# A linear-attention and long-convolution kernel: six batches' stores on GpSimd's queue, the first keys as fp32 by SyncE, sine's table first, three batches' keys and queries crossed

## The chip, the cores and the metric

The kernel runs on one core of a Trainium2 chip. Its metric is the device time in microseconds of one execution. The engines are named as in the profile: PE (TensorE's matrix products; PEld are its weight loads), DVE (VectorE), ACT (ScalarE), POOL (GpSimd) and SP (SyncE). POOL, SP and ACT can issue transfers (DMAs).

## What is computed

The reference has two stages. The first is an attention by random features, for 8 batches, 8 heads, 576 positions and 64 dimensions, with 128 features:

```python
def phi(x):
    proj = np.einsum('bhsd,md->bhsm', x, omega)
    sq = np.sum(x * x, axis=-1, keepdims=True) / 2.0
    h = proj - sq
    h = h - np.max(h, axis=-1, keepdims=True)
    return np.exp(h) / np.sqrt(m)
q_p, k_p = (phi(q_s), phi(k_s))
kv = np.einsum('bhsm,bhsd->bhmd', k_p, v)
z = np.sum(k_p, axis=2)
num = np.einsum('bhsm,bhmd->bhsd', q_p, kv)
den = np.einsum('bhsm,bhm->bhs', q_p, z)[..., None] + 1e-06
```

Its output num / den, as 8 x 576 x 512, goes through the second:

```python
proj = x @ w_proj
x1, x2, x3 = (proj[..., :D].copy(), proj[..., D:2 * D].copy(), proj[..., 2 * D:].copy())
X2 = np.fft.rfft(x2, n=S, axis=1)
H = np.fft.rfft(filter_fft, n=S, axis=0)[None, :, :]
x2_conv = np.fft.irfft(X2 * H, n=S, axis=1)
y = x1 * x2_conv * x3
return (y @ w_out).astype(np.float32)
```

All inputs and the output are fp32.

## The kernel before

Nearly all work is in bf16 tiles of 128 partitions. A batch's 576 positions are 512 main ones in four tiles (NT, SM) and 64 left ones (SL); the left ones of two batches share a tile. The kernel has two functions, `attention` (line 930) and `hyena` (1207), which loop over four pairs of batches.

**Attention, per batch.** Keys (`kn`), queries (`qn`) and values (`vn`) are loaded by POOL, whose DMAs cast fp32 to bf16 (`load_main`, 443; `load_left`, 467). Keys and queries must be turned so that the 64 dimensions lie on partitions. There are two ways. `transposes` (828) lets PE multiply by an identity, eight blocks of 128x128 in one PSUM bank `t`, and copies the bank out to `kt` or `qt`: on DVE for keys, on ACT for queries from batch 2. `cross` (950) has the DMA do it by one `dma_start_transpose` on SP. The name `crossed` (948) picks DMA for keys, queries and the attention's output (`xb4` to `xt`, 1163) of batches 4 to 7. The features are a product with `om2` and an exp on ACT (`ek`, `eqt`; `ekl`, `eql` for left ones); the sums `kv` and the normalised output, turned into `xt`, follow.

**Hyena, per pair.** The Fourier transform of length 576 is done as matrix products on folded data: `fold`, `project2`, `forward`, `spectrum` with `sw` and `xw` swapped between partition halves by SP's DMAs, `gates` (1247: x1 times x3 out of `xt` and `wproj`), `inverse`, and `out` (1469). In `out` a tile of 128 positions is four products with `wout`, an ACT copy into an fp32 tile `osb` (three buffers, which `inverse` uses as well), and a store of 256 KB by `nc.sync` (1506), or two of 128 KB for a pair's left positions (1509). The last pair's first eight tiles use other buffers (`spare`, 1461).

**The tables.** The transform's matrices are sines, made in the kernel. `make_residues` (562) takes two iotas of POOL (`pi`, the partition's number; `si`, 0 to 383, both integers), works out each partition's frequencies on DVE in small dependent steps (`fr`, its scale `fs`, signs `sg`, phases `ph`), then for three groups an ACT Identity (`yt`), a rounding on DVE, the residue `r`, and its signed maximum `ra`. `sines` (666) runs five ACT Sin instructions, `tables` (683) turns them on PE into `fwb`, `fwa`, `fwn`, `gtab` and others. The filter's own transform (771) follows. Sin and Exp need different ACT tables, so the loads go exp, sine, exp.

**The order.** No engine's instruction order is written out. `Plan` (110) records every operation with an assumed cost and a due time, which is counted back from its users and moved by the numbers in `LEAD`, `SHIFT` and `LEAN` (24 to 49). `simulate` (276) then steps through a model of engines, tile buffers and DMA queues and always takes, among what is ready first, the operation due earliest. `issue` (384) gives them out in that order, so all instructions carry line 390 in the profile. Each engine, the queues of POOL and SP among them, runs its own list strictly in order: an instruction that waits for a buffer holds whatever stands behind it.

Of the kernel before, what the change touches and what calls it, by code (L numbers as in the profile page):

```python
# [2 lines left out]

# [8 lines left out]
FP32 = mybir.dt.float32  # L12
BF16 = mybir.dt.bfloat16
FP16 = mybir.dt.float16
INT32 = mybir.dt.int32
# [7 lines left out]
PERIOD, STRETCH, STAY = 132.577, 8.076, 3059.83  # L23
LEAD = {
    "cross keys": -1.86, "cross out": 1.89, "cross queries": -0.95, "filter": -1.41,
    "fold": -1.38, "forward": 68.57, "gates": 0.52, "inverse": -1.95, "keys": 5.37,
    "left keys": -0.11, "left out": -0.33, "left queries": 37.06, "load filter": -63.41,
    "load k": -0.23, "load kl": -0.83, "load q": 0.19, "load ql": 1.42, "load v": 0.21,
    "load vl": -0.15, "load w0": -1.83, "load w1": 5.49, "load w2": 1.25, "out": -1.99,
    "queries": -0.43, "residues": 1.48, "rest": 0.66, "sines": 4.41, "start": -115.12,  # L30
    "sums": 37.58, "tables": -1.3, "turn out": -0.79, "turn queries": -0.04, "values": 96.58,
    "zeros": -0.01,
# [3 lines left out]
    ("fold", 0): -6.59, ("fold", 1): 51.34, ("forward", 1): -64.26, ("forward", 6): -65.11,  # L36
    ("forward", 7): -64.2, ("left keys", 2): 46.16, ("left queries", 7): -36.93,
    ("load kl", 0): -35.9, ("load q", 0): 1.17, ("load v", 0): -95.34, ("load v", 1): 95.91,
    ("load vl", 0): -20.54, ("out", 1): 148.99, ("queries", 1): 32.44, ("queries", 6): -10.06,
    ("rest", 1): 255.75, ("rest", 7): 5.08, ("sums", 2): -41.35, ("sums", 6): -35.91,  # L40
    ("sums", 7): -35.42, ("turn out", 1): 6.64, ("turn out", 2): -370.9,
    ("turn queries", 0): -3.89, ("turn queries", 2): 31.07, ("values", 0): -72.86,
    ("values", 1): 308.0, ("values", 2): -98.35,
}
LEAN = {
    ("fold", "DVE"): 3.25, ("forward", "PE"): 23.82, ("gates", "PE"): 78.43,
    ("keys", "PE"): -26.62, ("rest", "DVE"): 4.62, ("rest", "PE"): -3.97, ("start", "POOL"): 0.17,
    ("turn out", "DVE"): 4.04, ("turn queries", "DVE"): 13.21,
}

SIZE = {FP32: 4, INT32: 4, BF16: 2, FP16: 2, mybir.dt.uint32: 4}
# [58 lines left out]
class Plan:  # L110
# [86 lines left out]
    def _cost(self, op, eng, name, outs, ins):  # L197
# [6 lines left out]
        if name == "dma_start":  # L204
            a = out if out.space != bass.MemoryType.DRAM else ins[0]
            run = a.ap[-1][1] * SIZE[a.dtype]
            rows = a.ap[0][1] * self._free(a) // a.ap[-1][1]
            if eng == "POOL":
                op.busy, op.lat = (880.0 if rows > 600 else 720.0), 3300.0
                op.dma = ("SW", rows * max(run, 166) / 198.0)  # L210
            else:
                op.busy, op.lat = 580.0, 2000.0
                op.dma = ("HW", rows * run / 180.0 / (1 if out.space == bass.MemoryType.DRAM else 4))
            return
# [61 lines left out]
    def simulate(self):  # L276
# [16 lines left out]
        dma_free = {"SW": 0.0, "HW": 0.0}  # L293
        lanes = {"SW": [0.0] * 8, "HW": [0.0] * 8}
        for op in ops:
            if not op.deps:
                ready[op.eng].append(op)
        done, turn = [], {"SW": 0, "HW": 0}
        span, used, slow, half, table = 0, 0.0, True, False, "exp"
        while len(done) < len(ops):  # L300
# [46 lines left out]
            elif op.table and op.table != table:  # L347
                table = op.table
                busy, lat = busy + 1283.0, lat + 1283.0
            if op.dma:  # L350
                kind, serve = op.dma
                go = max(dma_free[kind], at + op.lat)
                if kind == "HW" and dma_free["SW"] > at:
                    go += 2500.0
                    if busy > 1000.0:
                        go, busy = go + 6000.0, busy + 4000.0
# [37 lines left out]
def kernel(  # L394
# [87 lines left out]
    pi_ = nc.tile(const, [P, 1], INT32, name="pi")  # L482
    si = nc.tile(hy, [P, 1024], INT32, name="x2", bufs=2)

    def first_constants():
        was, nc.where = nc.where, ("start", 0)
        nc.gpsimd.iota(pi_[:], pattern=[[1, 1]], base=0, channel_multiplier=1)
        nc.gpsimd.iota(si[:, 0 : 2 * CH], pattern=[[1, 2 * CH]], base=0, channel_multiplier=0)
# [3 lines left out]
    load_main(0, "k", 2, first_constants)  # L492
# [69 lines left out]
    def make_residues():  # L562

        sc = nc.tile(hy, [P, 2 * CH], FP32, name="xf", bufs=2)
        pf_ = nc.tile(const, [P, 4], FP32, name="pf")
        fr = nc.tile(const, [P, 4], FP32, name="fr")
        fl = nc.tile(const, [P, 2], FP32, name="fl")
        sg = nc.tile(const, [P, 2], FP32, name="sg")
        ph = nc.tile(const, [P, 3], FP32, name="ph")
        mk = nc.tile(const, [P, 2], FP32, name="mk")  # L570
        ts, tt = nc.vector.tensor_scalar, nc.vector.tensor_tensor
        stt = nc.vector.scalar_tensor_tensor
        p_ = fr[:, 0:1]
        nc.vector.tensor_copy(out=p_, in_=pi_[:])

        ts(out=pf_[:, 1:2], in0=p_, scalar1=63.5, scalar2=None, op0=ALU.is_ge)
        stt(out=pf_[:, 2:3], in0=pf_[:, 1:2], scalar=-64.0, in1=p_, op0=ALU.mult, op1=ALU.add)
        ts(out=mk[:, 1:2], in0=pf_[:, 2:3], scalar1=31.5, scalar2=None, op0=ALU.is_ge)
        ts(out=mk[:, 0:1], in0=mk[:, 1:2], scalar1=-1.0, scalar2=1.0, op0=ALU.mult, op1=ALU.add)
        stt(  # L580
            out=pf_[:, 3:4],
            in0=mk[:, 1:2],
            scalar=-32.0,
            in1=pf_[:, 2:3],
            op0=ALU.mult,
            op1=ALU.add,
        )
        ts(out=fr[:, 1:2], in0=pf_[:, 2:3], scalar1=128.0, scalar2=None, op0=ALU.add)
        ts(out=fr[:, 2:3], in0=pf_[:, 2:3], scalar1=3.0, scalar2=None, op0=ALU.mult)
        ts(out=fr[:, 3:4], in0=pf_[:, 3:4], scalar1=3.0, scalar2=192.0, op0=ALU.mult, op1=ALU.add)  # L590
        ts(out=fl[:], in0=fr[:, 0:2], scalar1=0.5, scalar2=-0.25, op0=ALU.mult, op1=ALU.add)
        ts(out=fl[:], in0=fl[:], scalar1=MAGIC, scalar2=-MAGIC, op0=ALU.add, op1=ALU.add)
        nc.vector.scalar_tensor_tensor(
            out=fr[:, 0:2], in0=fr[:, 0:2], scalar=1.0, in1=fl[:], op0=ALU.add, op1=ALU.add
        )


        ge2 = pf_[:, 1:2].to_broadcast([P, 2])
        ts(out=sg[:], in0=ge2, scalar1=2.0, scalar2=-1.0, op0=ALU.mult, op1=ALU.add)
        ts(  # L600
            out=ph[:, 0:2],
            in0=ge2,
            scalar1=-math.pi / 2,
            scalar2=math.pi / 2,
            op0=ALU.mult,
            op1=ALU.add,
        )
        nc.vector.memset(ph[:, 2:3], math.pi / 2)
        nc.vector.memset(fr[64:65, 2:3], 288.0)
        nc.vector.memset(sg[64:65, 1:2], -1.0)  # L610
        nc.vector.memset(ph[64:65, 1:2], math.pi / 2)
        zb = nc.tile(const, [P, 1], FP32, name="zb")
        nc.vector.memset(zb[:], 0.0)
        mg = nc.tile(const, [P, 1], FP32, name="mg")
        nc.vector.memset(mg[:], MAGIC)
        fs = nc.tile(const, [P, 4], FP32, name="fs")
        ts(out=fs[:], in0=fr[:], scalar1=1.0 / S, scalar2=None, op0=ALU.mult)
        nc.vector.tensor_copy(out=sc[:], in_=si[:, 0 : 2 * CH])

        for n, pieces in (  # L620
            (384, ((0, 0, 384),)),
            (384, ((1, 0, 384),)),
            (384, ((2, 0, 192), (3, 0, 192))),
        ):
            w = nc.tile(hy, [P, 1024], FP32, name="yt", bufs=2)
            r_ = nc.tile(hy, [P, 2, 1024], FP16, name="xt", bufs=4)
            kk = w[:, 0:n]
            r, ra = r_[:, 0, 0:n], r_[:, 1, 0:n]
            o = 0
            for c, lo, hi in pieces:  # L630
                nc.scalar.activation(
                    out=kk[:, o : o + hi - lo],
                    in_=sc[:, lo:hi],
                    func=AF.Identity,
                    scale=fs[:, c : c + 1],
                    bias=mg[:],
                )
                o += hi - lo
            ts(out=kk, in0=kk, scalar1=-MAGIC, scalar2=-float(S), op0=ALU.add, op1=ALU.mult)
            o = 0  # L640
            for c, lo, hi in pieces:
                os_ = slice(o, o + hi - lo)
                nc.vector.scalar_tensor_tensor(
                    out=r[:, os_],
                    in0=sc[:, lo:hi],
                    scalar=fr[:, c : c + 1],
                    in1=kk[:, os_],
# [3 lines left out]
                o += hi - lo  # L651
            c = pieces[0][0]
            for sgn, lo, hi in (
                ((-1.0, 0, 384),),
                ((sg[:, 0:1], 0, 384),),
                ((sg[:, 1:2], 0, 192), (sg[:, 0:1], 192, 384)),
            )[c]:
                nc.vector.scalar_tensor_tensor(
                    out=ra[:, lo:hi], in0=r[:, lo:hi], scalar=sgn, in1=r[:, lo:hi], op0=ALU.mult, op1=ALU.max
                )  # L660
# [269 lines left out]
    def attention():  # L930
        ekl = None
        for i in range(B // 2):
# [5 lines left out]
            for bb in range(2):  # L938
# [91 lines left out]
                for g in range(2):  # L1030

                    if not crossed:
                        turn_keys(g)
# [514 lines left out]
```

## Time and profile before

| What | Value |
|---|---|
| Median of 13 runs | 268.74 us (266.43 to 270.01) |
| Profiled execution, its own time | 268.26 us |
| Its span, first to last instruction | 266.4 us |
| Mean granted TensorE clock | 0.987 |
| POOL's queue (q0) | 59616 packets, 17.31 MB, 64.4% of 16 DMA engines' span |
| SP's queue (q1) | 33240 packets, 19.04 MB, 32.1% |
| HBM read / written | 34.64 / 9.44 MB |
| Stores issued by SP, 256 KB each, osb | 24, median 2.4 us from issue to landing |
| POOL's loads of left keys, values, queries (64 KB) / of 512 KB | 5.0 to 8.0 / 7.5 to 12.8 us to landing (medians by tensor) |
| ACT table loads | 3 of 1.28 us |

The profile is of one execution; all its times are microseconds from the span's start. A row of windows gives each engine's busy time and instruction count in one stretch. The chain of waits is followed back from the last instruction: at each step to what released it, or to the instruction before it on its engine. In the chain, "issue" is time for which the profile shows no reason. In a queue's timeline, the second number is the time that the issuing instruction held the queue, not the transfer's.

### The profile page before, as it was taken

The numbers are of one execution on the slowest core, as the hardware profiler recorded it, in microseconds if no ns is written. First come the engines' busy times: TensorE is split into PE (matmuls) and PEld (weight loads), VectorE is DVE, ScalarE is ACT, GpSimd is POOL, SyncE is SP. The second block draws the span as 40 slices with busy tenths as digits, with TensorE's granted clock in tenths as the row PEclk, the third lists the DMA queues.
The fourth block names the chain that finished last, engine by engine and source line by source line (L and its number), as shares of the span: only waits on it lengthen the run. The fifth ranks groups of instructions, "written<-read, shape, count | busy, mean of one in ns | idle before, by whom it ended". The sixth has DMA issues, their size and how long they took to land.

```text
span 266.4 us, 5662 instructions
## 1 busy us (share of the span) xinstructions
PE 238.6 (90%) x2171; PEld 135.2 (51%) x2202; DVE 214.9 (81%) x481; ACT 194.0 (73%) x304; POOL 62.7 (24%) x86
## 2 busy tenths in 40 slices
PE   0367979999999998997999799999999999999994
PEld 0255646655557455453754354544664554455541
DVE  7889894758896989997879795999989993476880
ACT  1897798469998998985666748996669637746433
POOL 8745631563463526320050000000000000000000
PEclk9996899999999999999999999999999999999999
DMA  6999999999999999899699927743418043302306
GB/s 76 189 196 170 190 218 223 181 169 146 160 150 148 198 153 85 157 194 213 125 119 178 177 51 201 112 158 90 90 31 244 8 102 134 81 20 61 139 0 197
DMA packets 93027, 36.83 MB, mean 138 GB/s; under 512 B 64460, under 2 KB 87497, under 8 KB 93001
## 3 DMA queue, kind: packets, MB, share of 16 engines
q0 software_dynamic: 59616, 17.31, 64.4%
q1 hardware_dynamic: 33240, 19.04, 32.1%
q8 instruction: 17, 0.28, 0.5%
q10 hardware_dynamic: 144, 0.13, 0.1%
q14 instruction: 10, 0.07, 0.1%
HBM read 34.64 MB, written 9.44 MB: 165 GB/s over the span
## 4 chain that ended last, share of the span: by engine, by line
PE 74%; ACT 10%; DVE 7%; DMA 5%; issue 3%; SPq 0%; ACTq 0%; DVEq 0%
PE h L390 57%; PE a L390 13%; PE t L390 4%; DMA out_dram<-osb 4%; ACT eqt L390 3%; ACT osb L390 2%; DVE h L390 1%; ACT L390 1%; ACT yt L390 1%; DVE vcl L390 1%; DMA xw<-xr 1%; DVE kt L390 1%; ACT gtab L390 1%; DVE x L390 1%; ACT x L390 0%
## 5 line engine op out<-in xcount | busy, mean ns | idle before, releaser
L390 PE MATMUL h<-xt,wproj 128*128 128x512 bf16 x245 | 60.2, 380 | 0.8 <-issue 0.3
L390 ACT CAST x<-h 128x512 bf16<-128x512 f32 x68 | 40.2, 600 | 24.7 <-PE h L390 23.4
L390 PEld LDWEIGHTS <-wproj 128*128 128x128 bf16 x384 | 31.0, 99 | 26.3 <-issue 2.3
L390 ACT ACTIVATE osb<-h 128x512 f32<-128x512 f32 (+4 forms) x49 | 27.6, 567 | 10.2 <-PE h L390 6.8
L390 ACT ACTIVATE ek<-a 128x1024 bf16<-128x1024 f32 x32 | 32.1, 1048 | 2.8 <-PE a L390 2.8
L390 ACT ACTIVATE eqt<-a 128x1024 bf16<-128x1024 f32 x32 | 32.7, 1051 | 1.6 <-PE a L390 1.4
L390 PE MATMUL h<-wout,yt 128*128 128x512 bf16 x124 | 30.7, 379 | 0.5 <-DVE yt L390 0.3
L390 PE MATMUL h<-wproj,xf 128*128 128x512 bf16 x122 | 30.3, 379 | 0.3 <-issue 0.2
L390 DVE TENSOR_TENSOR x<-h,x 128x512 bf16<-128x512 f32 x32 | 21.9, 685 | 6.1 <-PE h L390 4.6
L390 POOL DMA_DIRECT2D qn<-in_q_dram x26 | 22.9, 893 | 16.0 <-PE t L390 7.1
L390 PEld LDWEIGHTS <-yt 128*128 128x128 bf16 x128 | 12.2, 98 | 14.9 <-DVE yt L390 0.8
L390 PE MATMUL h<-x,fwb 128*128 128x512 bf16 x68 | 18.1, 379 | 1.8 <-ACT osb L390 1.5
L390 PEld LDWEIGHTS <-xf 128*128 128x128 bf16 x134 | 12.4, 100 | 12.7 <-issue 0.5
L390 DVE TENSOR_TENSOR bt<-h,osb 128x384 f16<-128x384 f32 x32 | 17.0, 553 | 2.2 <-ACT osb L390 1.3
L390 PE MATMUL h<-gtab,xs 128*128 128x384 bf16 x64 | 15.6, 325 | 2.4 <-ACT x L390 1.2
L390 DVE TENSOR_TENSOR xf<-xt 128x1024 bf16<-128x1024 bf16 (+1 forms) x16 | 8.7, 552 | 7.5 <-ACT xt L390 4.6
L390 PEld LDWEIGHTS <-eqt 128*128 128x128 bf16 x256 | 11.3, 98 | 5.4 <-ACT eqt L390 0.6
L390 DVE TENSOR_TENSOR xb<-a,rden 128x512 bf16<-128x512 f32 x20 | 13.2, 676 | 0.3
L390 PE MATMUL a<-qt,om 64*128 64x512 bf16 x64 | 11.7, 397 | 1.8 <-DVE qt L390 1.0
L390 PE MATMUL a<-om,kt 64*128 64x128 bf16 x256 | 11.8, 226 | 1.7 <-DVE kt L390 1.0
L390 PE MATMUL a<-kv,eqt 128*128 128x65 bf16 x256 | 12.6, 194 | 0.5 <-ACT eqt L390 0.5
L390 POOL DMA_DIRECT2D vn<-in_v_dram x8 | 7.2, 902 | 24.9 <-DVE x13l L390 14.2
(168 smaller groups left out, 471.4 us busy)
## 6 DMA issues: line engine op xcount, KB each, us to landing
out_dram<-osb SPq DMA_DIRECT2D x24, 256.0 KB, 2.4
vn<-in_v_dram POOLq DMA_DIRECT2D x8, 512.0 KB, 9.4
kn<-in_k_dram POOLq DMA_DIRECT2D x7, 512.0 KB, 7.5
qn<-in_q_dram POOLq DMA_DIRECT2D x24, 128.0 KB, 9.4
sw<-sp SPq DMA_DIRECT2D x16, 128.0 KB, 2.4
wproj<-in_moe_w_proj_dram POOLq DMA_DIRECT2D x3, 512.0 KB, 12.8
qn<-in_q_dram POOLq DMA_DIRECT2D x2, 512.0 KB, 10.3
out_dram<-xf SPq DMA_DIRECT2D x4, 256.0 KB, 2.0
```

The costliest lines, as they stand in the source:

```text
L390: getattr(real, name)(*args, **kw)
```

## The change

There are four edits, and new numbers for the planner.

1. **Stores.** `store(b)` picks the queue of each output store: POOL's for batches 0 to 5, SP's for 6 and 7. These are 30 of the 41 stores.
2. **First keys.** Batch 0's keys no longer come through POOL. SP loads them as fp32 in two halves into `k32`, which takes a buffer of `ek`; DVE casts the first half to bf16, ACT the second.
3. **Residues and sine's table.** A Sin of one column on a zeroed tile, due at the start, lets the sine table be loaded first. POOL's iotas now give the frequencies themselves in fp32 (`fi`, by a multiplier of 3 per partition), so that most of the small steps, the casts and the signs go. Where the maximum took |r| for some partitions, the sign bit is now cleared in place, by a bitwise and on the fp16 bits.
4. **Crossing.** The three turns have bounds of their own: keys and queries cross from batch 5, the output from batch 4 as before. Batch 4's keys and queries are turned on PE.
5. **Planner.** All lead times are new, and its model of the DMA queues has a kind for SP's loads, longer times for a transpose issued near POOL's loads, and no table at the start.

```diff
+CROSSED = {"keys": 5, "queries": 5, "out": 4}
...
-        nc.gpsimd.iota(pi_[:], pattern=[[1, 1]], base=0, channel_multiplier=1)
-        nc.gpsimd.iota(si[:, 0 : 2 * CH], pattern=[[1, 2 * CH]], base=0, channel_multiplier=0)
+        iota = partial(nc.gpsimd.iota, allow_small_or_imprecise_dtypes=True)
+        iota(fi[:, 0:1], pattern=[[1, 1]], base=1, channel_multiplier=3)
+        for r in (slice(0, 64), slice(64, 128)):
+            iota(fi[r, 1:3], pattern=[[-385, 2]], base=385, channel_multiplier=3)
+        iota(si[:, 0 : 2 * CH], pattern=[[1, 2 * CH]], base=0, channel_multiplier=0)
...
-    load_main(0, "k", 2, first_constants)
+    def first_keys():
+        nc.at("load k", 0)
+        k32 = nc.tile(att, [P, H, NT, D], FP32, name="ek", bufs=2)
+        t_ = nc.tile(nat, [P, H, NT, D], BF16, name="kn", bufs=2)
+        for g in range(2):
+            hs = slice(4 * g, 4 * g + 4)
+            nc.sync.dma_start(
+                out=k32[:, hs].rearrange("p h t d -> p h (t d)"),
+                in_=k[0, hs, 0:SM, :].rearrange("h (p t) d -> p h (t d)", t=NT),
+            )
+        for g in range(2):
+            hs = slice(4 * g, 4 * g + 4)
+            if g == 0:
+                nc.vector.tensor_copy(out=t_[:, hs], in_=k32[:, hs])
+            else:
+                nc.scalar.copy(out=t_[:, hs], in_=k32[:, hs])
+        nat_tiles["k", 0] = t_
+
+    first_keys()
+    first_constants()
...
+        nc.at("start", 0)
+        nc.vector.memset(zb[:], 0.0)
+        sn = nc.tile(const, [P, 1], FP32, name="sn")
+        nc.scalar.activation(out=sn[:], in_=zb[:], func=AF.Sin)
+        nc.at("residues", 0)
...
+        nc.vector.tensor_tensor(out=fi[:, 3:4], in0=fi[:, 2:3], in1=kc[:], op=ALU.add)
+        nc.vector.memset(fi[64:65, 2:3], 288.0)
+        ts(out=fs[:], in0=fi[:], scalar1=1.0 / S, scalar2=None, op0=ALU.mult)
+
+        def unsigned(o, x):
+            ts(
+                out=o.bitcast(UINT16),
+                in0=x.bitcast(UINT16),
+                scalar1=0x7FFF,
+                scalar2=None,
+                op0=ALU.bitwise_and,
+            )
...
+            if c == 0:
+                unsigned(ra, r)
+            else:
+                unsigned(r[lo64], r[lo64])
+            if c == 2:
+                row = r[64:65, 0:n]
+                unsigned(row, row)
...
-                crossed = b >= B // 2
+                crossed = {n: b >= first for n, first in CROSSED.items()}
...
+            def store(b):
+                return nc.gpsimd if b < B - 2 else nc.sync
...
-                        nc.sync.dma_start(out=out[b, t * P : (t + 1) * P, :], in_=osb)
+                        store(b).dma_start(out=out[b, t * P : (t + 1) * P, :], in_=osb)
                     else:
                         for j in range(2):
-                            nc.sync.dma_start(
+                            store(b).dma_start(
                                 out=out[2 * i + j, SM:S, :], in_=osb[j * SL : (j + 1) * SL, :]
                             )
```

## The prediction, made before the changed kernel ran

> **What bounds the kernel now.** I read the page first: busy time by engine and the slices.
>
> ```profile
> PE 238.6 (90%) x2171; PEld 135.2 (51%) x2202; DVE 214.9 (81%) x481; ACT 194.0 (73%) x304; POOL 62.7 (24%) x86
> ...
> PE   0367979999999998997999799999999999999994
> ...
> PEclk9996899999999999999999999999999999999999
> ```
>
> TensorE is busy 238.6 of 266.4 us, so 27.8 us are idle. The slices put most of that at the left edge. The windows (us; busy and count of PE, PEld, DVE, ACT, POOL; clock; DMA share; GB/s) say how much:
>
> ```profile
> 0.00:10.00 10.00, 0.90 (x5) 0.50 (x6) 7.53 (x38) 3.42 (x5) 7.75 (x17) 1.00 0.99 112
> 10.00:20.00 10.00, 5.93 (x79) 4.74 (x80) 8.68 (x28) 9.73 (x13) 6.02 (x10) 1.00 1.49 195
> 20.00:30.00 10.00, 8.22 (x108) 6.04 (x107) 9.82 (x22) 6.75 (x8) 7.12 (x10) 0.66 1.31 176
> 30.00:40.00 10.00, 8.04 (x79) 4.78 (x80) 8.89 (x16) 9.65 (x17) 3.31 (x5) 1.00 1.28 210
> ...
> 120.00:140.00 20.00, 18.38 (x223) 11.79 (x224) 15.89 (x34) 12.33 (x23) 4.38 (x5) 1.00 1.02 153
> 140.00:160.00 20.00, 18.38 (x129) 9.08 (x130) 17.91 (x40) 12.53 (x20) 0.00 (x0) 1.00 0.91 137
> ```
>
> PE's idle time is 9.10 + 4.07 + 1.78 + 1.96 = 16.9 us up to 40 us, and 1.62 + 1.62 = 3.2 us between 120 and 160. The last 26.4 us hold 4.3 us (22.07 busy), mostly the last tile's way out. That leaves 27.8 - 16.9 - 3.2 - 4.3 = 3.4 us for all the rest: elsewhere every nanosecond of PE work counts. So two places can be shortened, the start and 120 to 160, and whatever is added to PE after 44 us is paid in full. Next, the chain of waits up to 44 us:
>
> ```profile
> 6.88 1.31 ACT yt L390 x2
> ...
> 9.17 0.99 ACT yt L390 x2
> 10.16 0.02 issue
> 10.18 1.28 ACT L390
> 11.46 0.01 issue
> 11.47 1.63 ACT gtab L390 x3
> ...
> 13.81 1.28 ACT L390
> 15.10 1.03 ACT ekl L390
> ```
>
> The two ACT pieces of 1.28 us without a tile are the loads of sine's table and then of exp's, the second and third of three. The first exp of the attention, ekl, cannot start before 15.10, behind the residues and sines. Then DVE carries the chain to 24.7, PE at half clock to 29.2 and ACT to 41. Ahead of 6.88 the chain is DVE alone, through the residues' small instructions down to fs. Last, for 120 to 160, the SP queue and the chain:
>
> ```profile
> 116.07 2.95 SPq L390 DMA_TRANSPOSE kt<-kn  x1
> 119.12 1.77 SPq L390 DMA_DIRECT2D out_dram<-osb  x2
> ...
> 137.88 6.69 SPq L390 DMA_TRANSPOSE xt<-h  x1
> 144.66 0.53 SPq L390 DMA_DIRECT2D out_dram<-osb  x1
> ```
>
> Both stores stand behind a transpose whose issue holds SP for 2.95 and 6.69 us. In the chain they take 5.72 and 5.31 us to land, ACT then waits 1.77 and 1.84 us for a free osb, and the timeline shows PE idle behind that for 1.46 us before 125.86 and for 0.25 + 1.24 us before 152.60. That is 2.95 us of PE.
>
> **The change, part by part.** Residues: today the scales wait for an iota, a cast and about fifteen dependent DVE instructions, 3.76 to 6.85 us. After it three remain after the iotas (add, one memset, scale), 3 x 0.17 = 0.5 us by today's rows. The iotas cost POOL 3 x 0.16 + 0.5 us. If they go first on POOL, right after ident (1.3 us), ACT's first yt can start at 2.9. If loads go ahead of them as now (iota of x ends at 4.41), at 4.9. Today 6.88: a gain of 2.0 to 4.0. One table load of the three goes, because sine's takes the place of the exp load at 0.74, when ACT had nothing to do: 1.28 us out of the chain. The four fp16 scalar_tensor_tensor instructions that take |r| (0.55 + 0.61 + 2 x 0.41 = 2.0 us on DVE) become short bit operations, about 0.8 us at the 0.2 us of DVE's smallest ops here: 1.2 us less, beside ACT's work.
>
> First keys: two SP loads of 512 KB each, fp32. Today kn of batch 0 stands third on POOL (issued 4.3 to 6.8) and PE still waits for it at 9.98. SP was free from 1.14, and the windows give the DMA only 15 and 27 GB/s in the first two 2 us, so the megabyte moves into bandwidth that is idle, and POOL's other loads follow earlier. At the 190 GB/s of 10 to 20 us and 2 us to land, the halves are there at about 6 and 8.5 at worst. The casts are new. ACT's half costs what the COPY of 128x1024 costs, 1.04 us. It lies in the ACT chain, or, if keys come before the sines' input, in ACT's wait before it. DVE's half is 0.6 to 1.1 us (0.35 us for the 384-wide fp32 cast today), about what |r| gives back.
>
> Sum of the start: -(2.0 to 4.0) - 1.28 + (0 to 1.04), so -2.2 to -5.3. What follows may not take it all: gates start at 43.75, and wproj, the last of their inputs by DMA, lands at 43.35 (POOL's wait for it ends there). wproj should move up with the queue by the 1 MB of fp32 keys that leaves it, at the 2 x 195 GB/s that a casting queue reads (the page has q0 at 17.31 MB and HBM reads at 34.64) about 2.7 us. I take -3.5. Lower end -1.5 (DMA holds), upper -5.
>
> Stores of batches 0 to 5: 30 issues leave SP (median 0.50 us each) and go to POOL, whose issues cost 0.69 (64 KB) to 0.89 us (512 KB). 30 x 0.75 = 22 us on an engine that is 24% busy: no bound. Landing decides. The 64 KB POOL loads take 5.0 to 8.0 us, beside 2.4 us for an SP store, so a 256 KB store is between 3 (queue empty, after 145 us) and 8 us (loads ahead of it). The first store was written at 116.39 and ACT wanted its buffer at 123.17; the second at 140.60 and 148.23. At 5.5 us from the write they land at 121.9 and 146.1, and both waits are gone; at 8 us, 1.2 and 0.4 remain. So -2.95 to -1.4; I take -2.6. Against this stands a rule of the Trainium skill (DMA: Bandwidth & Descriptors, Rules for kernel authors): spreading DMAs over SP, ACT and GpSimd doesn't help, since all run on the same engines and only issue time is saved. By it the term is 0 and the forecast 2.6 us higher. But the row shows that issue time is what is lost: 2.7 and 4.1 us between the write and SP's turn. I go by the row. A second rule (SBUF — State Buffer, "DVE blocks DMA" trap) says that a GpSimd DMA of 620 ns takes about 3100 beside a two-port DVE copy, 30 x 2.5 = 75 us on POOL. POOL's issues here are 0.88 to 0.89 us at 87% DVE load in 60 to 100 us, so I charge nothing.
>
> Batch 4 turns keys and queries on PE again (crossing starts at 5; out still from 4). That is 4 groups of 8 transposes of 0.45 to 0.62 us: +1.8 to +2.5, in full, because PE idles 0.9 us in 60 to 100. DVE gets two copies of 0.68, ACT two of 1.04. ACT idles 2.05 us in 60 to 100, so 2.1 more just fills it, up to +1.0. The two transposes that leave SP (67.17 and 94.37) issued in 1.44 and 1.32 us and no compute engine waited for them: 0. I take +2.2 for all.
>
> The new order of all instructions (other lead times) removes no work. Outside start, stores and tail it has 3.4 us of PE idle to win, and I know no limit on what it may lose: 0, with -1.5 to +2.
>
> Sum: -3.5 - 2.6 + 2.2 = -3.9. Its own time was 268.26 (span 266.4 plus 1.9 around it), so 264.4; the median, 0.48 higher, gives **264.8**.
>
> **Rivals.** (a) Start in full and the order closes more gaps: -5 - 2.95 + 1.8 - 1.0 = -7.1, so 261.6. For it: DVE's chain ahead of 6.88 really vanishes and the half-clock stretch (22 to 29 us) may shrink. Against: wproj. (b) DMA holds the start: gates still begin near 43 whatever ACT does. -1.0 - 2.6 + 2.2 = -1.4, so 267.3; with 1.2 more on ACT in 60 to 100, 268.5, no change. For it: the DMA moves about 200 GB/s without a pause from 6 to 50 us. (c) Slower: POOL's queue is in order, and its loads wait for buffers, once 14.18 us (vn for the x13l on DVE, ending 132.69) and once 6.62 (kn for the transpose, ending 110.68). A store queued behind such a load keeps osb shut. In 116 to 125 ACT bore 6.8 us from write to landing. Behind a 6.62 us wait and 5.5 to land it is 12.1, or 5.3 of stall, in place of 2.6 saved: -3.5 + 5.3 + 2.2 = +4.0, so 272.7; behind the long one more. It turns the sign once the stalls exceed 1.3 us, a store 8.1 us late. Against it: POOL's order is set by due times and modelled buffer releases, so a load should go in only when its slot is about to open, and after 137 POOL has no loads. (d) The stores' move saves nothing, since landing is slower by what issue gains: -3.5 + 2.2 = -1.3, so 267.4, same range as (b).
>
> **Chances.** Forecast 0.50 (262.7 to 266.8), (a) 0.20, (b) and (d) together 0.15, (c) 0.15. About 0.5%, 1.3 us, is what can be told from no change. (b) and (d) lie on that edge: 0.05 of them count as faster and 0.10 as same. (c) is slower: faster 0.75, same 0.10, slower 0.15. The range runs from (a)'s lower half, 259.5, to past (b), 269.5.
>
> **What would show it.** Right: one table load less, first exp near 11.5 us, gates near 40, PE idle before 40 us near 13.5, no ACT wait on out_dram over 0.5 us, SP's stores only at the end, PE busy near 240.7. Wrong: gates still near 43 (b); POOL's stores idle behind slot waits and ACT waiting on out_dram for several us (c); PE gaps of more than 0.5 us in 60 to 110 that end on ACT (batch 4's copies dearer than put here).

## The result, and the profile after it

| Kernel | Median | Profiled execution, its span |
|---|---|---|
| before | 268.06 us (48 runs) | 268.26, 266.4 us |
| changed | 269.96 us (11 runs, 269.27 to 272.71) | 269.59, 267.8 us |

The ratio is 1.0109 (95% interval 1.0077 to 1.0141): slower by 1.1%, or 2.9 us of 268.06. It lies above the 0.7% between the two medians because it leaves out slower executions, into which the kernel before falls now and then. Below, the microseconds of a run are its ratio less one, times 268.06. The forecast was 264.8, so its sign was wrong.

The page of the changed kernel, the same three lines as before:

```profile
PE 241.5 (90%) x2202; PEld 135.9 (51%) x2234; DVE 213.5 (80%) x475; ACT 195.0 (73%) x307; POOL 77.9 (29%) x116
...
PE   0587689999998999997999999999999999999994
...
PEclk9999999999999999999999999999999999999999
```

PE has 2.9 us more busy time, and idles 26.3 us in place of 27.8. The two stretches that the prediction wanted shorter (columns as before):

```profile
0.00:10.00 10.00, 0.90 (x5) 0.58 (x6) 8.01 (x34) 6.39 (x10) 9.25 (x20) 1.00 1.00 182
10.00:20.00 10.00, 9.11 (x101) 6.59 (x100) 9.42 (x29) 8.48 (x10) 3.37 (x5) 1.00 1.46 198
20.00:30.00 10.00, 6.72 (x128) 5.00 (x128) 9.74 (x19) 7.01 (x9) 4.25 (x7) 1.00 1.50 194
30.00:40.00 10.00, 8.12 (x105) 5.25 (x105) 7.80 (x16) 8.99 (x13) 6.39 (x9) 1.00 1.30 202
...
120.00:140.00 20.00, 17.99 (x139) 8.98 (x139) 12.38 (x29) 11.72 (x19) 6.87 (x10) 1.00 1.26 182
140.00:160.00 20.00, 19.84 (x179) 11.41 (x181) 15.87 (x37) 12.72 (x24) 0.77 (x2) 1.00 0.38 73
```

From 10 to 20 us PE is busy 9.11 us (5.93 before), and from 20 to 30 6.72 (8.22). In the second window it does more in less time, 128 recorded products for 108, because the kernel before runs there at a granted clock of 0.66. So busy time does not measure progress here. From 140 to 160 the waits are gone (0.16 us idle, 1.62 before); from 120 to 140 they have grown (2.01, 1.62 before).

The chain of waits ends after 19 pieces in this profile, so the start is read from ACT's timeline (start, duration, instruction; in brackets the idle time ahead of it and what ended it):

```profile
0.74 1.28 ACT L401 ACT_TABLE_LOAD   x1 [0.74 <-PEq L1534]
...
3.79 1.31 ACT L401 ACTIVATE yt<-x,mg,fs 128x384 f32<-128x384 f32 x2 [1.56 <-DVE ph L401]
5.36 1.04 ACT L401 CAST kn<-ek 128x1024 bf16<-128x1024 f32 x1 [0.26 <-DMA ek<-in_k_dram]
...
11.23 0.45 ACT L401 ACTIVATE x<-xt,ph 128x192 bf16<-128x192 f16 x1 [2.27 <-DVE xt L401]
...
12.05 1.28 ACT L401 ACT_TABLE_LOAD   x1
13.35 1.02 ACT L401 ACTIVATE ekl<-a 128x1024 bf16<-128x1024 f32 x1
```

There is one table load less, and the first yt is 3.1 us earlier (3.79 for 6.88). Then ACT casts keys for 1.04 us and waits 2.27 us for DVE's xt. The first exp, ekl, comes 1.75 us earlier (13.35 for 15.10), not at 11.5. Short windows of the same kernel show what follows:

```profile
26.00:28.00 2.00, 1.81 (x41) 1.50 (x38) 1.97 (x3) 0.59 (x1) 0.52 (x1) 1.00 1.37 201
28.00:30.00 2.00, 0.99 (x14) 0.61 (x13) 1.97 (x7) 0.58 (x1) 0.90 (x1) 1.00 1.24 205
30.00:32.00 2.00, 1.42 (x20) 0.80 (x18) 1.97 (x4) 1.09 (x3) 1.09 (x2) 1.00 1.24 203
```

DVE (third pair of numbers) has no gap, and ACT (fourth) idles more than half of the time. I read this as a start that hangs on DVE's total work, which the change leaves as it was (34.96 us up to 40, 34.92 before); e4 below puts it to the test. Last, PE's longest gap after 44 us, and ACT and POOL's queue ahead of it:

```profile
123.64 0.81 PE L401 MATMUL h<-wproj,xf 128*128 128x512 bf16 x3 [1.90 <-ACT osb L401]
```

```profile
122.72 0.48 ACT L401 CAST osb<-h 128x384 f16<-128x384 f32 x1 [1.90 <-DMA out_dram<-osb]
```

```profile
115.32 0.59 POOL L401 DMA_DIRECT2D out_dram<-osb  x1 [0.23 <-issue]
```

PE waits for ACT's osb, and ACT waits 1.90 us for a store to land. That store was issued at 115.32, behind four loads of 64 KB, and landed at 122.62, 7.3 us later. The next store, at 117.96 behind two loads of 512 KB, took 10.6 us, but no engine is seen to wait for it.

### The profile page after: what moved, and what is told of

It is laid out like the page before. It is cut to its first block, busy times and chain, and to the rows that moved or that the text cites. A ratio compares the mean times of both kernels' runs of the same rounds, so it can differ in the third digit from the quotient of the medians.

```text
span 267.8 us, 5733 instructions
## 1 busy us (share of the span) xinstructions
PE 241.5 (90%) x2202; PEld 135.9 (51%) x2234; DVE 213.5 (80%) x475; ACT 195.0 (73%) x307; POOL 77.9 (29%) x116
## 5 line engine op out<-in xcount | busy, mean ns | idle before, releaser
L401 PE MATMUL h<-xt,wproj 128*128 128x512 bf16 x245 | 60.9, 380 | 0.9 <-ACT osb L401 0.2
L401 POOL DMA_DIRECT2D out_dram<-osb x30 | 16.5, 550 | 109.6 <-ACT osb L401 109.4
L401 DVE TENSOR_TENSOR bt<-h,osb 128x384 f16<-128x384 f32 x32 | 16.4, 552 | 9.0 <-ACT osb L401 8.6
L401 PE MATMUL a<-kv,eqt 128*128 128x65 bf16 x256 | 12.3, 194 | 1.3 <-DVE xb L401 0.9
L401 PEld LDWEIGHTS <-kt 64*128 64x128 bf16 x256 | 7.6, 96 | 9.1 <-issue 6.6
```

The source lines that it names most:

```text
L401: getattr(real, name)(*args, **kw)
```

## The experiments

The planner turns every edit into a new order of all instructions. So there are three kinds of runs. In some, only an operation's engine is changed where it is issued, and the order stays. In some the planner plans anew. And in some the order is held: the planner's simulation is left out, each operation keeps the time that the plan of before (or of the changed kernel) gave it, and only operations that an edit adds get a place by hand.

```diff
-                at, op = min(
-                    ((at, op) for at, op in cands if at <= soon),
-                    key=lambda c: (c[1].due - STAY * (half and c[1].rows == 64), c[1].n),
-                )
+            op.start = KEYS[k][i]
...
+            ready.sort(key=lambda o: (o.start, o.n))
```

| Run | Order | Ratio to before (95%) | us |
|---|---|---|---|
| changed kernel | its own | 1.0109 (1.0077 to 1.0141) | +2.9 |
| e1: 30 stores on POOL | before's | 1.0165 (1.0107 to 1.0223) | +4.4 |
| g1: 20 of them, batches 2 to 5 | before's | 1.0044 (0.9987 to 1.0102) | +1.2 |
| h1: new start | before's | 0.9930 (0.9892 to 0.9968) | -1.9 |
| h2: batch 4 turned on PE, late | before's | 1.0442 (1.0374 to 1.0510) | +11.8 |
| h5: the same, early | before's | 1.0364 (1.0309 to 1.0420) | +9.8 |
| h3: all edits, turns late | before's | 1.0343 (1.0247 to 1.0439) | +9.2 |
| h6: all edits, turns early | before's | 1.0341 (1.0275 to 1.0407) | +9.1 |
| v1: start, 20 late stores on POOL | before's | 0.9940 (0.9903 to 0.9978) | -1.6 |
| v2: start, 10 first stores by ACT | before's | 0.9913 (0.9867 to 0.9960) | -2.3 |
| e2: changed, all stores by SP | changed's | 1.0278 (1.0234 to 1.0321) | +7.5 |
| e3: changed, batch 4's qt on DVE | changed's | 1.0081 (1.0059 to 1.0104) | +2.2 |
| e4: changed, batch 1's qt on ACT | changed's | 1.0090 (1.0063 to 1.0118) | +2.4 |
| k1: changed, batch 4 by DMA | changed's | 1.0046 (1.0010 to 1.0083) | +1.2 |
| k2: changed, 10 first stores by ACT | changed's | 1.0110 (1.0055 to 1.0166) | +2.9 |
| f0: changed, before's lead times | planned anew | 1.1790 (1.1706 to 1.1873) | +48 |
| f1: changed, batch 4 by DMA | planned anew | 1.0689 (1.0587 to 1.0791) | +18.5 |
| f2: before, changed's lead times | planned anew | 1.0722 (1.0636 to 1.0807) | +19.4 |
| f4: before's lead times, new start | planned anew | 1.0697 (1.0632 to 1.0762) | +18.7 |

### The stores: e1, e2, g1, k2

```diff
+        if stage == "out" and b < 6 and name == "dma_start":
+            real = nc.gpsimd
```

e2 has `nc.sync` there, g1 `2 <= b < 6`, and k2 `b < 2` with `nc.scalar`.

> The kernel before with one thing changed: the 30 output stores of batches 0 to 5 are issued by GpSimd, each at the place in the program where SyncE issued it. Every other engine's order is the one of before. If moving stores is the gain that was put at 2.6 us (waits of 1.77 and 1.84 us of ScalarE on out_dram gone): 265 to 266.5 us, ratio about 0.991, and no wait of ScalarE on out_dram over 0.5 us. If GpSimd's stores are themselves what made the changed kernel slower (a store behind a load that waits for its buffer): 269 us or more, with new waits of several us on out_dram. If the stores were never worth anything (the landing is slower by what the issue gains): 268, ratio 1.000 within 0.3%.

> The changed kernel with one part undone at the point of issue: all stores by SyncE, in the changed kernel's own order. If GpSimd's queue is worth 1.3 to 2.6 us also in the new order: 271 to 272.5, ratio to before 1.015 to 1.024, with SyncE's stores waiting behind transposes near 92 to 107 us and ScalarE waiting on out_dram there. If GpSimd's stores are the cause of the loss: faster than the changed kernel, 268.5 or less, ratio 1.002 or less. If they are neutral: 270, ratio 1.011.

> The kernel before, every engine's order unchanged, with only the stores of batches 2 to 5 issued by GpSimd (20 of 30); those of batches 0 and 1 stay on SyncE. Theory now (a store on GpSimd is late only behind loads in the same queue, and after 137 us there are none): 266.5 to 268.0 us, since the 1.24 us wait for a buffer before 152.60 may go. Rival (a store costs more on GpSimd's queue wherever it stands): +2 to +4, 270 to 272.

> The changed kernel with its own order, and only the stores of batches 0 and 1 issued by ScalarE instead of GpSimd; those of batches 2 to 5 stay on GpSimd. Theory now (two of these stores land 7 to 11 us late behind loads, and cost TensorE the 1.9 us gap before 123.6): ratio to before 1.002 to 1.006. Rival (the gap moves to the next thing that is late): 1.009 to 1.012.

The stores alone cost 4.4 us in before's order, where the prediction had -2.6. PE's gap ahead of one product of the inverse transform tells it, first in before and then in e1:

```profile
125.86 0.81 PE L390 MATMUL h<-x,fwb 128*128 128x512 bf16 x3 [1.46 <-ACT osb L390]
```

```profile
128.22 0.81 PE L391 MATMUL h<-x,fwb 128*128 128x512 bf16 x3 [3.92 <-ACT osb L391]
```

That single gap is 2.46 us longer. ACT's write of the tile and POOL's queue in e1 say why:

```profile
115.69 0.60 ACT L391 ACTIVATE osb<-h 128x512 f32<-128x512 f32 x1
```

```profile
117.56 0.89 POOL L391 DMA_DIRECT2D vn<-in_v_dram  x1 [3.19 <-DVE vc L391]
118.44 0.59 POOL L391 DMA_DIRECT2D out_dram<-osb  x1
```

The store goes out at 118.44, 0.7 us before SP's in the kernel before (119.12), but behind a load that had waited 3.19 us for its buffer. It lands at 127.20, 8.8 us from its issue and 10.9 from the write. SP's landed at 124.84 (5.7 us from issue). Behind the gap, eleven products take 3.96 us for 2.53, at a granted clock of 0.65 from 128 to 132 us. The other wait that the prediction named, 1.24 us before 152.60, is gone in e1, as foreseen. In all the profiled span is 3.0 us longer; the rest of the median's 4.4 I can't place. g1 puts only the stores after the last loads on POOL: +1.2, with zero inside its interval. The difference to e1, 1.2%, is the ten stores of batches 0 and 1, which have loads around them.

In the new order the opposite holds: SP in place of POOL costs 4.5 us more (ratios 1.0278 and 1.0109). Lines of e2's SP and PE:

```profile
115.28 3.21 SPq L402 DMA_TRANSPOSE qt<-qn  x1
118.58 2.04 SPq L402 DMA_DIRECT2D out_dram<-osb  x2
```

```profile
127.40 1.44 PE L402 MATMUL h<-wproj,xf 128*128 128x512 bf16 x3 [4.30 <-ACT osb L402]
```

The store that PE's product waits for was written at 116.38. It stands behind a transpose that holds SP until 118.49, and lands at 126.37, 7.8 us from its issue. So the 1.90 us gap becomes 4.30. This is the loss of issue time that the prediction meant to end.

My guess for k2 was wrong: by ACT the ten stores are as dear as by POOL, +2.9. ACT's queue has no loads in it, yet in v2 (below) a store that ACT issued at 138.28 took 7.4 us to land. In k2's trace, which is of its longest execution (274.27 us), the store at 115.61 that PE's product waits for took 9.5. So loads ahead in the store's own queue are not needed for a late landing. Common to these cases is that POOL's loads and a transpose of SP are under way; which of them delays the store no run here parts.

### The start: h1, f4

Edits 2 and 3 in before's order; f4 plans the same anew.

> The kernel before with its own instruction order on every engine, and only edits 2 and 3 in it: first keys as fp32 by SyncE, frequencies by iota, sine's table first. Only the instructions that these edits replace are new or gone; each stands where the plan of the changed kernel puts it. Stores, batch 4's crossing and all the rest are as before. Theory now (the start is bound by VectorE's total work, so most of what ScalarE gains is lost waiting): 266.7 us, 1.4 less than before, PE idle before 40 us near 15.5. Rival 1 (the prediction's term, -3.5): 264.6, PE idle near 13.5. Rival 2 (an order fitted to one program punishes any edit): 268.5 or more.

> Only the start of the change (first keys as fp32 by SyncE, iotas in fp32 and sine's table first), with the stores, the crossing and the lead times of the kernel before, planned anew. If the start is worth the forecast 3.5 us: 264.5, ratio 0.987. If it is worth the 1.4 us that the two traces show by 40 us: 266.6, ratio 0.995. If the lead times suit only the program they were fitted to: 269 or more, with the start itself earlier in the trace (first exp before 14 us) and the time lost after 60 us.

h1 is faster by 1.9 us (0.9 to 2.9), so -3.5 is outside and -1.4 inside. Both kernels run the same PE order, so one product can be followed. In before and in h1:

```profile
40.93 0.19 PE L390 MATMUL a<-vcl,ekl 128*128 128x65 bf16 x1 [0.33 <-ACT eqt L390]
```

```profile
40.34 0.19 PE L675 MATMUL a<-vcl,ekl 128*128 128x65 bf16 x1 [0.33 <-ACT eqt L675]
...
124.36 0.81 PE L675 MATMUL h<-x,fwb 128*128 128x512 bf16 x3 [0.63 <-ACT osb L675]
```

ekl starts 2.1 us earlier in h1 (12.98), yet at 40 us only 0.59 is left. Most of that is not the start but the granted clock from 22 to 29 us, 0.51 in before and 0.76 in h1. h5 and g1 have before's program up to there, at 0.76 and 0.91. The window in before and in g1, then the product in h5 and in g1:

```profile
22.00:29.00 7.00, 6.02 (x76) 4.49 (x75) 6.87 (x15) 5.10 (x6) 5.71 (x8) 0.51 1.30 165
```

```profile
22.00:29.00 7.00, 5.58 (x92) 3.87 (x86) 6.87 (x15) 6.41 (x8) 6.04 (x8) 0.91 1.28 167
```

```profile
40.53 0.19 PE L671 MATMUL a<-vcl,ekl 128*128 128x65 bf16 x1 [0.33 <-ACT eqt L671]
```

```profile
39.97 0.19 PE L391 MATMUL a<-vcl,ekl 128*128 128x65 bf16 x1 [0.33 <-ACT eqt L391]
```

At the same clock the new start is ahead by 0.2 us: h1 at 40.34 for h5's 40.53, and v1 (0.92) at 39.77 for g1's 39.97. The profiled span of h1 is 3.6 us shorter (262.8), and most of that is in shorter waits for stores past 120 us: the gap of 1.46 us is 0.63, and the one before 152.60 is gone, though no store was moved. The median's -1.9, which v1 and v2 repeat, is the size to trust; by what path the start earns it is not shown. f4 tells nothing of the start.

### Batch 4's turns: h2, h5, k1, f1, e3, e4

> The kernel before with its own order, and only batch 4's keys and queries turned on TensorE: 32 transposes more, two copies more on VectorE and two on ScalarE, each put some 1 to 3 us ahead of its first reader in the plan of before; two DMA transposes less on SyncE. Theory now and the prediction's term agree on +2.2 to +2.7 for TensorE's own time: 270.6 us. Rival 1 (the copies hold ScalarE in its full stretch as well): +3.5 to +4.5, 272. Rival 2 (the DMA transposes that go were stopping loads, so landings come sooner): +1.0, 269.

> As the kernel with batch 4's turns alone in before's order, but the same transposes and copies stand where before had its two DMA transposes (keys near 69 us, queries near 94 us), 10 to 20 us ahead of their use; GpSimd's order is again that of before. Theory now (the turns were dear because kn and qn were held until they were used, and the loads of batches 5 and 6 went out up to 20 us late): the load of kn goes out near 84 us again, and the time is before's plus TensorE's 2.2 to 2.7: ratio 1.008 to 1.012, 271 us. Rival 1 (the copies on VectorE and ScalarE hold up the rest wherever they stand): ratio 1.02 or more. Rival 2 (the landings come sooner without the DMA transposes): 1.000 to 1.005.

> The changed kernel with its own order on every engine, but batch 4's keys and queries crossed by DMA transposes on SyncE again; the transposes stand where the plan had the first of TensorE's turns. Theory now (the turns cost in the new order at least TensorE's own 2.2 to 2.5 us, and their copies hold ScalarE): ratio to before 0.998 to 1.003, 8 us or so below the run with the same edit planned anew. Rival (the new order was made around turns, and two more DMA transposes hold SyncE and stop the loads near 65 and 95 us): 1.015 or more.

> The changed kernel with one edit undone: keys and queries of batch 4 cross by DMA again, planned anew with the changed kernel's own numbers. If batch 4's turns on TensorE cost the 2.2 to 3.6 us that the comparison of the two traces puts on 60 to 100 us: 266.4 to 268, ratio 0.994 to 1.000. If the two more DMA transposes stall GpSimd's loads and stores[...]: 271 or more, ratio over 1.013.

In before's order the turns cost 11.8 us, where both the prediction and my later theory had 2.2 to 2.7. h2 puts them a few us ahead of their use, and PE then waits for their copies; POOL's load of kn, which needs the buffer that they read, goes out at 103.11 (83.50 in before). Lines of h2's PE and POOL:

```profile
108.60 0.61 PE L671 MATMUL t<-ident,xb 128*128 128x128 bf16 x8 [1.48 <-ACT qt L671]
...
133.93 1.14 PE L671 MATMUL h<-x,fwb 128*128 128x512 bf16 x3 [2.25 <-ACT osb L671]
```

```profile
103.11 0.89 POOL L671 DMA_DIRECT2D kn<-in_k_dram  x1 [4.08 <-PE h L671]
```

h2 also shows what PE's busy time is worth. Its first 40 us are the program of before, and the same eight transposes take longer in it, both at a granted clock of 1.00 from 18 to 22 us. In before and in h2:

```profile
20.20 0.61 PE L390 MATMUL t<-ident,kn 128*128 128x128 bf16 x8 [1.24 <-DVE kt L390]
```

```profile
20.57 1.01 PE L671 MATMUL t<-ident,kn 128*128 128x128 bf16 x8 [0.78 <-DVE kt L671]
```

h5 puts the same instructions where the DMA transposes stood. The load goes out at 83.08 again, yet the time is +9.8. My explanation by the held buffer thus covers at most 2 us, and the intervals of h2 and h5 overlap. PE in h5:

```profile
70.86 0.61 PE L671 MATMUL t<-ident,kn 128*128 128x128 bf16 x8 [0.76 <-ACT qt L671]
73.95 0.61 PE L671 MATMUL t<-ident,kn 128*128 128x128 bf16 x8 [0.67 <-ACT qt L671]
```

The turns themselves now wait for ACT, and PE's strict order makes everything behind them wait. These gaps and two more near 100 us (0.36 and 0.26) add 2.05 us; with PE's own work and what follows, h5's profiled span is 5.9 us longer than that of before. The rest of the median's 9.8 I can't place.

k1 takes the turns out of the new order: +1.2 in place of +2.9, so there they cost 1.7 us (0.4 to 3.0), close to the predicted 2.2. The turns' price is 1.7 in an order made for them and 10 to 12 in one that is not.

> The changed kernel with batch 4's two copies of turned queries out of PSUM moved from ScalarE to VectorE, nothing else. If the loss of TensorE between 80 and 90 us (2.1 us of lost time there in the changed kernel, 0.5 in the kernel before) comes from ScalarE being full with batch 4's copies: 0.5 to 1.3 us faster than the changed kernel, 268.7 to 269.4, ratio about 1.004 to 1.008, and TensorE's idle time in 80 to 100 us down from 1.6 to below 1.0. If that loss has another cause (order[...]): as the changed kernel, 270, ratio 1.011.

> The changed kernel with batch 1's two copies of turned queries moved from VectorE to ScalarE, nothing else. They lie at 25.8 and 27.7 us, where VectorE is 98% busy and ScalarE 29%. If the start is bound by the sum of VectorE's work (34.9 of the first 40 us in both kernels), 1.4 us less of it makes the kernel 0.7 to 1.4 us faster than the changed one: 268.6 to 269.3, ratio 1.003 to 1.008. If the start is bound by the weights' DMA or by ScalarE: no change or up to 1 us slower, 270 to 271, ratio 1.011 or more.

```diff
+        if (stage, b, name) == ("turn queries", 4, "copy"):
+            real, name = nc.vector, "tensor_copy"
```

Both moves of a copy (e4 sends batch 1's from DVE to ACT) are within 0.7 us of the changed kernel. The gaps between 80 and 90 us (0.52 and 0.27, ended by ACT's eqt) stay with e3, so batch 4's copies don't make them.

e4 is also the test of the start: if DVE's total work binds it, 1.4 us less of that should gain 0.7 to 1.4. The same product in e4 and in the changed kernel, both at a clock of 1.00 from 22 to 32 us:

```profile
37.70 0.23 PE L402 MATMUL a<-vcl,ekl 128*128 128x65 bf16 x1
```

```profile
38.33 0.23 PE L401 MATMUL a<-vcl,ekl 128*128 128x65 bf16 x1
```

It comes 0.6 us earlier (38.39 in k1, at the same clock), which speaks for DVE, but less than the work moved, and the time (1.0090) can't be told from the changed kernel's 1.0109. So DVE's part is made likely, not shown.

### All edits and the order: h3, h6, f0, f2

> All edits of the change at once (start, batch 4's turns on TensorE, 30 stores on GpSimd), but in the order of before: the planner's new lead times are left out. Theory now (in one order the edits add up: -1.4 +2.5 +4.4): 273.6 us, so that the new order gives back some 3.6 us of what the edits cost. Rival 1 (the prediction's terms for start and turns, with the +4.4 measured for the stores alone): 271.2. Rival 2 (the stores' cost belongs to the DMA transposes of batch 4 that hold the loads ahead of them; with those gone the stores are free): 269.2.

> All edits of the change in before's order, as in the run of that kind, but batch 4's turns stand early. Theory now (the edits add up once no buffer is held): start -1.9, turns +2.4, stores +4.4: ratio 1.018, 273 us. Rival 1 (with two DMA transposes less, the stores of batches 0 and 1 no longer come late): ratio 1.002 to 1.008. Rival 2 (the edits still hinder one another): 1.03 as in the run with late turns.

> All edits of the change, but the planner's lead times (and its period) are those of the kernel before; the order is planned anew from them. If the edits are worth what was forecast and the new order throws it away: 264 to 266 us, ratio about 0.985. If each edit has its own price whatever the order (start 1.4 us earlier, batch 4 dearer by 3.6, stores about even): 269 to 270.5, as the changed kernel. If an order only suits the program that its numbers were fitted to: 272 or more, ratio 1.015 or more.

> The kernel before, with no edit of the change but the new lead times of the planner. If the order alone made the loss: 270 to 271, ratio 1.008 to 1.012. If an order only suits the program that its numbers were fitted to: 273 or more. If order is nearly neutral and the edits make the loss: 267.5 to 269.

In before's order all edits together cost 9.2 or 9.1 us; with its own order the change costs 2.9. So the new order is worth about 6 us to the changed program (3.6 to 9.0 by h3). Nor do the edits add up: -1.9 + 4.4 + 9.8 or 11.8 gives 12.3 or 14.3, some 3 to 5 us more; the 3 lies at the edge of the noise, the 5 beyond it. And lead times made for one program, planned for another, cost 18 to 48 us against before. An edit that is planned anew is buried under that; the four f runs tell of the planner, not of an edit.

### Better than both: v1, v2

> Before's order with the new start, and only the stores of batches 2 to 5 on GpSimd; batch 4 still crossed by DMA. Theory now (start -1.9, late stores 0 to +1.2): ratio 0.990 to 0.998, 265 to 268 us. Rival (the stores behind a transpose on SyncE near 144 us are late by 4 us in before, and now are not): ratio 0.985.

> Before's order with the new start, and the stores of batches 0 and 1 issued by ScalarE, which writes the tile that they store; those of later batches on SyncE as before. They then stand behind neither a transpose nor a load. Theory now (a store is late only by what stands ahead of it in its queue): the two waits of ScalarE for osb between 116 and 152 us go, -1.0 to -2.9, against ten issues of some 0.5 us on ScalarE in a stretch where it is two thirds busy: ratio 0.983 to 0.992, 263 to 266 us. Rival 1 (a store beside GpSimd's loads lands late whichever queue it is in): as with the start alone, ratio 0.993. Rival 2 (the issues hold up ScalarE's copies): ratio 1.000 or more.

Both beat the kernel before, at 265.24 and 264.21 us, and so the changed one. Their intervals overlap h1's: the new start in the old order is what is shown to pay, and neither move of stores adds anything that these runs can tell. In v2 the 1.46 us gap of PE is gone, but ACT issued two of its stores only at 122.57 and 123.22, later than SP did, so my reason for it (no queue ahead) isn't what the trace shows.

## Why the prediction was wrong, step by step

- **"PE's idle time ... 16.9 us up to 40 us ... two places can be shortened"**: the places were right, the measure was poor. In h2 the first 40 us are the program of before. PE is busy 25.38 us there and 23.09 in before, yet the product above starts at 40.97 and 40.93. The 2.3 us are slower instructions, not more work (0.61 and 1.01 us for the same eight transposes, above). So the 15.15 us of idle in the changed kernel, 1.75 less than before, can't be read as a gain either.
- **Start, "I take -3.5"**: over-sized. One table load less and the earlier yt came as foreseen. The step that failed took ACT's chain for the path: ekl starts 2.1 us earlier in h1, and 0.2 of that is left at 40 us. In the changed kernel ACT waits for DVE, 98% busy from 20 to 36 us; that DVE is the path instead is likely, not shown (e4). In before's order the start is worth -1.9. Gates begin at 42.99 (43.75), as rival (b) had it, but the wait ahead of them ends on DVE's xf (0.43 us), not on wproj. For rival (a) the prediction named the half-clock stretch: it is gone in the changed kernel, and by g1 it cost the kernel before 1.0 us.
- **Stores, "I take -2.6"**: wrong in sign in before's order (+4.4), and right in sign in the new one, where SP costs 4.5 more than POOL (e2). The failing step in before's order is "at 5.5 us from the write they land". It was 10.9 us in e1, past the 8.1 at which rival (c) saw the sign turn, behind a load that had waited for its buffer, as (c) had it. The rule that the prediction set aside speaks of bandwidth; read as 0 it was off as well. Nor was it only issue time that made the two waits: in h1, which moves no store, one shrank by 0.83 us and the other went. In the changed kernel the store that PE waits for landed 7.6 us from its write and cost 1.90 us, and the wait between 140 and 160 went: 1.1 us of PE idle saved there in all, not 2.6.
- **Turns, "+2.2 for all"**: right in the new order (1.7), by luck of the order: in before's, which it was read from, +9.8 to +11.8. "No compute engine waited for them: 0" for the two DMA transposes is where it failed, since what takes their place must be waited for (0.76 and 0.67 us in h5).
- **"The new order ... removes no work ... 0, with -1.5 to +2"**: wrong by 6 us in one direction, and the edits by 13 in the other (+9.2 for -3.9). This is the step that decided: I added costs read in the old order and put the order at 0. What the runs show in its place is that an edit's price depends on the order: 1.7 or some 10 us for the turns, +4.4 or -4.5 for the stores.

What stays open: the changed kernel without turns is still +1.2 (k1), though the start alone gives -1.9 in before's order. Those 3.1 us belong to stores and order together; the runs don't part them. Why a store lands late, and how the start comes to be worth -1.9 when 0.2 us are left of it at 40, are open too. And h2 and h5 are two places for the turns out of many; a better one in before's order was not tried.

## What to carry to other kernels

Where a planner writes the order, an edit's price is that of edit and order together: measure the edit with the order held, and the order with the edits held, before adding anything up. An instruction that leaves a waiting queue (a DMA) for a strictly ordered busy engine brings its waits with it. A store's landing depends on what transfers are under way at that microsecond, whichever of the three engines issues it, so look there and not at the engine's share of busy time. Before two traces are compared by busy or idle time, compare the clock, and follow one instruction.

## What the runs showed of the hardware that was not expected

- One DMA transpose held SP for 1.32 us (at 94.37) to 6.69 us (at 137.88) in the kernel before. (The second number of a row of a queue's timeline is a hold only in a row of x1; one of x2 spans both instructions and the time between them.)
- 256 KB stores on POOL's queue took 2.3 us to land at best, 10.6 at worst, in the changed kernel. On ACT's queue, with no load in it, one took 7.4 (v2), and on SP's one took 8.1 (before, at 137.07).
- A granted clock of 0.51 from 22 to 29 us cost the kernel before 1.0 us at 41 us: g1, the same program up to there at 0.91, reaches the product at 39.97 for 40.93.
- A granted clock of 1.00 does not mean equal speed: eight transposes took 0.61 us in before and 1.01 in h2. The traces show no reason.
